# Values projected eight heads at a time, a second row chunk turned by TensorE, and another split of the exponentials

## The chip, the cores and the metric

The kernel runs on one core of one Trainium2 chip. The metric is device time in microseconds (us), from runs of the whole kernel. The core has a matrix engine (TensorE, PE in the profile), a vector engine (VectorE, DVE), a scalar engine (ScalarE, ACT), a general engine (GpSimd, POOL) and a sync engine whose queue issues most transfers (SyncE, SP). Tensors live in SBUF, 128 partitions wide; PE writes its results to PSUM, 8 banks of 512 float32 columns per partition.

## The reference, cut to what matters

The input x has 2048 rows of 512. Two attention layers read it, each with 32 heads of 16 columns, and a gate mixes them.

```python
g = sigmoid((x * gate_w).sum(-1, keepdims=True))
# A: linear attention with a feature map
phi(t) = concat(softmax(t @ w_phi), softmax(-t @ w_phi))     # per head, 16 -> 32
a = (phi(q) @ (phi(k).T @ v)) / (phi(q) @ sum(phi(k)) + 1e-6) @ A_wo
# B: softmax attention over all 2048 keys
b = softmax(q @ k.T * 0.25) @ v @ B_wo
return g * a + (1 - g) * b
```

Nearly all of the work is B's softmax: 32 heads x 2048 x 2048 exponentials.

## The kernel before, in words

**Sets and steps.** B is done in 32 sets: four chunks of 512 query rows, in each four groups of eight heads, in each group the even and the odd heads. A set goes through 16 tiles of 128 keys (a step each). For a step PE makes scores in two pairs of matmuls (L752), each pair 128 keys x 1024 columns in PSUM; then the scores are turned into exponentials, and PE multiplies these by the values (four matmuls of 32 columns of values, L794 or L807), summing in the PSUM tile O. The values of a head stand in `vB` as 16 columns and two columns of ones, so that the sum of the exponentials comes out beside the product.

**Two ways to an exponential.** On ACT one activation makes 1024 columns (L771), so a step costs two of them. On DVE a step is two conversions of scores to an integer form (L761, "di"), a mask (L777, "dm"), a multiply (L780, "dw") and a second mask (L784, "de"); the result is two parts, D's F and I tiles, and each is multiplied by the values. `NDVE` (L35) says for each of the 32 sets how many of its 16 steps DVE takes: 117 of 512 in all. In sets 0 and 1 it is one step each.

**What else is done.** Keys and queries of B are projected by groups of eight heads (`k_proj` L488, `q_proj` L500), four matmuls of 512 columns each (`fill`, L471, helper line L475), then copied out of PSUM. Queries are spread into four zero-padded copies: the first by four DVE multiplies with masks (L510), later ones by eight small transfers each on SP's queue (L521), into buffers that POOL clears at the start (L446). Values of B are projected for all 32 heads at once (`v_proj` L525): four matmuls of 512 columns for each tile of 128 rows, two tiles side by side in one of the three 1024-column PSUM tiles R, which the scores use too, and DVE copies both out at once (L469, 128x1024). All eight such pairs of tiles come before or in set 0 and early in set 1. A's part runs between: the gate (L593), folded weights (L613), phi of the keys for 16 row tiles (two ACT exponentials L634, a DVE sum L636 and reciprocal L640, a POOL multiply L641), then the products of keys and values (L665), then phi of the queries for 16 row tiles with numerator and denominator (L690 to L703). At the end of each set O is copied out (L828), turned by PE (L835) and divided (L840, L841). Output rows are made in `of`/`os` (L891, L899) and scaled (L907).

**The start.** x must stand transposed in SBUF as `xT`. Its first 512 rows come by a plain transfer (L405) and are turned by sixteen PE matmuls against an identity (L550); ACT copies one half out of PSUM (L553), DVE the other (L554). The other three chunks of 512 rows come by transposing transfers on SP's queue (L409), one after another. Weights come on ACT's queue in five transfers (L412 to L416), that of the values whole, in third place.

**What sets the order.** Every operation is added to a planner (`_Sched`, L90) with an engine, a priority, a duration of its own and what it depends on. `run` (L148) places operations one by one on a model of the engines; the order that comes out is the fixed program order of each engine, and waits on semaphores are put in from the dependencies. Priorities are times: `ut(u)` (L459) turns a place in the plan (32 units a set, 1024 in all) into a time, from `NDVE`. Constants such as `RUSH`, `HOLD`, `STAY`, `KLEAD`, `QLEAD`, `EARLY` (L47 to L61) shift priorities; `next_pe` (L117) picks PE's next operation, scores for ACT first when ACT has few ahead. Phi of the keys starts at unit 100, 16 units a tile (L648); the keys' products stand at 360, phi of the queries at 400, 32 units a tile (L681); output rows of a query chunk at 545 and on, 128 apart (L886).

Of the kernel before, what the change touches and what calls it, by code (L numbers as in the profile page):

```python
# [6 lines left out]
BF16 = mybir.dt.bfloat16  # L7
# [26 lines left out]
VROW = H * VW + 16  # L34
NDVE = [1, 1, 4, 4, 4, 3, 4, 4, 3, 4, 3, 4, 4, 3, 5, 4, 4, 3, 4, 3, 5, 3, 4, 4, 5, 3, 4, 4, 4, 3, 5, 4]  # L35
# [11 lines left out]
STAY = 1.0  # L47
PAIRS = (0, 1, 2, 3, 4, 5, 6, 7)
# [12 lines left out]
EARLY = 8.0  # L61
# [268 lines left out]
def _build(ctx, nc, A_x, A_wqkv, A_w_phi, A_wo, B_wqkv, B_wo, gate_w, out):  # L330
# [19 lines left out]
    vB_ = sb([128, NT, VROW], name="vB")  # L350
    vB = vB_[:, :, 0:H * VW].rearrange("p t (h c) -> p t h c", c=VW)
    vA = sb([128, NT, 8, 66], name="vA")
# [51 lines left out]
    xs = D_all[0].bitcast(BF16).rearrange("p (i c) -> p i c", c=D)  # L404
    op_x0 = dma("sp", -100, 3.6, xs, A_x[0, 0:NQ, :].rearrange("(i p) c -> p i c", p=128), name="x0")  # L405
    op_x = [None]
    for c in range(1, QC):
        op_x.append([add("sp", -100 + c, 2.5,
                         lambda e, c=c: e.dma_start_transpose(xT[:, :, NQ * c:NQ * (c + 1)], A_x[0, NQ * c:NQ * (c + 1), :]),  # L409
                         name=f"x{c}", dma=7.0)])  # L410
# [3 lines left out]
    op_wv = dma("act", -98, 6.0, W_Bv[:], wbv[:, :, 2 * D:3 * D], name="wv")  # L414
    op_wk1 = dma("act", -97, 8.0, W_Bk[:, :, 128:D], wbv[:, :, D + 128:2 * D], name="wk")
    op_wq1 = dma("act", -96, 8.0, W_Bq[:, :, 128:D], wbv[:, :, 128:D], name="wq")  # L416
    op_wat = add("sp", -90, 3.0, lambda e: e.dma_start_transpose(WAT[:], A_wqkv[:, 0:2 * D]), name="wat", dma=3.0)
# [22 lines left out]
    op_vpad = [pool(-99, 0.2, lambda e: e.memset(vB_[:, :, H * VW:VROW], 0.0), name="vpad")]  # L440
# [59 lines left out]
    def q_proj(g, c, prio, tile, off):  # L500
# [4 lines left out]
        if (g, c) == (0, 0):  # L505
# [3 lines left out]
            for j in range(4):  # L509
                ms.append(add("dve", prio + 0.01 * j, 0.39, lambda e, j=j: e.tensor_scalar(  # L510
                    qt.ap[:, j, :], q3(), masks[:, j:j + 1], None, op0=ALU.mult),
                    deps=[ev, op_masks] + (ms if j == 3 else []), tiles=[qt], name=f"qm{g}{c}{j}"))
            ev_q[g, c] = ms
# [11 lines left out]
    def v_proj(st, n, prio):  # L525

        tile = _Tile(M_r if n == 1 else R_r)
        fs = [fill(prio, tile, 512 * i, lambda t, i=i: xT[:, t, 128 * (st + i):128 * (st + i + 1)], lambda t: W_Bv[:, t, :],
                   op_x[st // 4] + [op_wv], f"vf{st}") for i in range(n)]
        use_wv.extend(fs)  # L530
        src = lambda: tile.ap[:, 0:512 * n].rearrange("p (t h d) -> p t h d", t=n, d=16)
        e1 = evac("dve", prio, lambda: vB[:, st:st + n, :, 0:16], src, fs, [tile], n=512 * n, name=f"vev{st}")
        for i in range(n):
            ev_v[st + i] = e1
# [7 lines left out]
    tx = _Tile(R_r)  # L542
    txv = lambda: tx.ap.bitcast(BF16).rearrange("p (t q) -> p t q", q=NQ)
    xtp = []
    for t in range(KT):

        def fn(e, t=t):
            ins = None
            for i in range(4):
                ins = e.transpose(txv()[:, t, 128 * i:128 * (i + 1)], xs[:, i, 128 * t:128 * (t + 1)], ident[:])  # L550
            return ins
        xtp.append(add("pe", -80 + t, 0.3, fn, deps=[op_x0, op_id], tiles=[tx], mode="full", name="xtp"))
    op_x[0] = [add("act", -80, 0.9, lambda e: e.copy(xT[:, 0:2, 0:NQ], txv()[:, 0:2, :]), deps=xtp[0:2], tiles=[tx], name="xev"),  # L553
               add("dve", -80, 0.6, lambda e: e.tensor_copy(xT[:, 2:4, 0:NQ], txv()[:, 2:4, :]), deps=xtp[2:4], tiles=[tx], name="xev")]  # L554
    I_r.tenant[0] = _Tile(None)
    I_r.tenant[0].ops = xtp
    tq = _Tile(R_r)
    k_proj(0, 0, -50, tq, 0, "act")
    q_proj(0, 0, -49, tq, 512)
    tk1 = _Tile(R_r)  # L560
# [4 lines left out]
    for st in range(0, NT, 2):  # L565
        if st // 2 in PAIRS:
            v_proj(st, 2, ut(2 * st) - VLEAD)
        else:
            v_proj(st, 1, ut(2 * st) + 0.5)
            v_proj(st + 1, 1, ut(2 * st + 2) + 0.5)  # L570
# [76 lines left out]
    for st in range(NT):  # L647
        prio = ut(100 + 16 * st)  # L648
# [9 lines left out]
    for lo, hi in ((0, 4), (4, 8)):  # L658
        tkv = _Tile(M_r)
        kvo = []  # L660
        for g in range(lo, hi):
# [6 lines left out]
            kvo.append(add("pe", ut(360 + 3 * g), 0.5, fn, deps=op_phk + ev_vA + kvo[-1:], tiles=[tkv], mode="full", name="kv"))  # L668
        kvw = lambda tkv=tkv: tkv.ap[:, 0:260].rearrange("p (g c) -> p g c", c=65)
        op_kz.append(add("dve", ut(384), 0.334, lambda e, kvw=kvw, lo=lo, hi=hi: e.tensor_tensor(  # L670
            kz[:, lo:hi, 0:64], kvw()[:, :, 0:64], mask64[:].unsqueeze(1).to_broadcast([128, 4, 64]), ALU.mult),
            deps=kvo + [op_m64], tiles=[tkv]))
        op_kz.append(add("dve", ut(384), 0.1, lambda e, kvw=kvw, lo=lo, hi=hi: e.tensor_tensor(
# [3 lines left out]
    op_woA = dma("sp", ut(400), 4.0, WoA, A_wo.rearrange("(t p) c -> p t c", p=128), deps=op_kz, name="woA")  # L677
    op_woB = dma("sp", ut(400), 4.0, WoB, B_wo.rearrange("(t p) c -> p t c", p=128), deps=op_kz, name="woB")
# [421 lines left out]
```

## Time and profile before

| what | value |
|---|---|
| median of 3 runs | 791.6 us (791.0 to 792.72) |
| the profiled execution's own time | 790.62 us |
| its span, first to last instruction | 788.8 us |
| ACT busy | 764.3 us, 97% of the span |
| DVE busy | 710.5 us, 90% |
| PE busy | 708.3 us, 90% |
| POOL busy | 121.1 us, 15% |
| mean granted clock of PE | 0.998 of full speed |
| scores to exponentials on ACT (L771) | 790 activations of 1024 columns |
| steps on DVE (L777, one each) | 117 |
| value projection: copies out of PSUM | 8, 1225 ns each |

Busy time counts each engine's own instructions, in one profiled execution; what an engine waits for is put down to the instruction whose end released it. Consecutive instructions of one engine overlap in their records, so that the time from one start to the next is shorter than one duration. The span leaves out 1.8 us of the execution's own time. A line number is a line of the kernel, and several operations recorded by one helper share its line.

### The profile page before, as it was taken

The numbers are of one execution on the slowest core, as the hardware profiler recorded it, in microseconds if no ns is written. First come the engines' busy times: TensorE is split into PE (matmuls) and PEld (weight loads), VectorE is DVE, ScalarE is ACT, GpSimd is POOL, SyncE is SP. The second block draws the span as 40 slices with busy tenths as digits, with TensorE's granted clock in tenths as the row PEclk, the third lists the DMA queues.
The fourth block names the chain that finished last, engine by engine and source line by source line (L and its number), as shares of the span: only waits on it lengthen the run. The fifth ranks groups of instructions, "written<-read, shape, count | busy, mean of one in ns | idle before, by whom it ended". The sixth has DMA issues, their size and how long they took to land.

```text
span 788.8 us, 13621 instructions
## 1 busy us (share of the span) xinstructions
PE 708.3 (90%) x5645; PEld 224.7 (28%) x5716; DVE 710.5 (90%) x883; ACT 764.3 (97%) x865; POOL 121.1 (15%) x123
## 2 busy tenths in 40 slices
PE   8899999999999898998888999899998999988886
PEld 3223232222222222332222323222232232222222
DVE  2456999999999999999999999999999999999993
ACT  4989999999999999999999999999999999999995
POOL 7000002022233322111112010310111101120000
PEclk9999999999999999999999999999999999999999
DMA  9100000000000000023110121210111101120000
GB/s 240 28 8 2 11 4 1 10 6 1 14 1 8 9 1 14 1 68 41 28 21 21 30 19 34 48 23 19 27 22 40 35 14 27 35 42 1 7 1 30
DMA packets 55923, 19.57 MB, mean 25 GB/s; under 512 B 48304, under 2 KB 55856, under 8 KB 55856
## 3 DMA queue, kind: packets, MB, share of 16 engines
q1 hardware_dynamic: 52960, 17.06, 10.4%
q10 hardware_dynamic: 2640, 1.57, 0.7%
q8 instruction: 46, 0.75, 0.4%
q14 instruction: 21, 0.17, 0.1%
q0 software_dynamic: 256, 0.02, 0.0%
HBM read 3.69 MB, written 2.10 MB: 7 GB/s over the span
## 4 chain that ended last, share of the span: by engine, by line
ACT 87%; PE 6%; DVE 4%; DMA 2%; SPq 1%; issue 0%
ACT E L771 80%; ACT WAT L634 4%; PE ps L752 2%; ACT phiK L771 2%; PE ps L475 1%; DVE D L761 1%; DMA xT<-in_A_x_dram 1%; ACT vA L771 1%; PE ps L891 1%; PE ps L807 1%; SPq L521 1%; DVE D L777 1%; DVE D L780 1%; SPq L409 1%; PE ps L665 0%; DMA WB<-WB 0%
## 5 line engine op out<-in xcount | busy, mean ns | idle before, releaser
L771 ACT ACTIVATE E<-ps 128x1024 bf16<-128x1024 f32 x766 | 713.2, 1185 | 4.3 <-PE ps L807 2.2
L752 PE MATMUL ps<-q,kT 64*128 64x512 bf16 x2048 | 362.8, 385 | 58.1 <-ACT E L771 45.7
L761 DVE TENSOR_SCALAR D<-ps 128x1024 int16<-128x1024 f32 x234 | 284.5, 1216 | 21.7 <-PE ps L752 21.1
L752 PEld LDWEIGHTS ps<-q,kT 64*128 64x128 bf16 x2048 | 89.8, 93 | 275.2 <-ACT E L771 214.3
L807 PE MATMUL ps<-E,vB 128*32 128x512 bf16 x1532 | 149.1, 389 | 5.0 <-issue 4.3
L780 DVE TENSOR_TENSOR D<-D 128x2048 bf16<-128x2048 bf16 x117 | 141.4, 1209 | 0.6
L794 PE MATMUL ps<-D,vB 128*32 128x512 bf16 x936 | 90.8, 386 | 1.6 <-issue 1.0
L638 POOL TENSOR_TENSOR acc<-acc,ss 128x64 f32<-128x64 f32 x32 | 24.9, 778 | 435.4 <-DVE ss L636 435.4
L777 DVE TENSOR_SCALAR D<-D 128x2048 int16<-128x2048 int16 x117 | 83.8, 717 | 1.1
L784 DVE TENSOR_SCALAR D<-D 128x2048 int16<-128x2048 int16 x117 | 81.7, 698 | 0.1
L807 PEld LDWEIGHTS ps<-E,vB 128*32 128x32 bf16 x1532 | 37.8, 93 | 85.4 <-issue 77.5
L475 PE MATMUL ps<-xT,WB 128*128 128x512 bf16 x111 | 40.2, 388 | 3.3 <-ACT WAT L634 1.4
L634 ACT ACTIVATE WAT<-ps 128x512 bf16<-128x512 f32 x64 | 39.6, 755 | 0.0
L636 DVE TENSOR_REDUCE ss<-WAT 128x64 f32<-128x1024 bf16 x32 | 38.8, 1212 | 0.6 <-ACT WAT L634 0.4
L475 PE MATMUL ps<-Wp,xT 128*128 128x512 bf16 x98 | 38.0, 389 | 0.5 <-DVE OT L469 0.3
L641 POOL TENSOR_TENSOR phiK<-WAT,ss 128x1024 bf16<-128x1024 bf16 x16 | 35.6, 2222 | 10.7 <-DVE ss L640 10.7
L641 POOL TENSOR_TENSOR WB<-WAT,ss 128x1024 bf16<-128x1024 bf16 x16 | 33.5, 2096 | 14.3 <-DVE ss L640 14.3
L794 PEld LDWEIGHTS ps<-D,vB 128*32 128x32 bf16 x936 | 23.7, 94 | 37.5 <-issue 29.0
L469 DVE CAST vB<-ps 128x1024 bf16<-128x1024 f32 x8 | 9.8, 1225 | 22.0 <-PE ps L475 22.0
L835 PE MATMUL ps<-ident,OT 128*128 128x128 f32 x128 | 27.6, 300 | 0.5 <-ACT WAT L634 0.3
L891 PE MATMUL ps<-phiK 128*128 128x512 bf16 x74 | 25.8, 386 | 0.8 <-issue 0.3
L848 POOL TENSOR_TENSOR acc<-acc,rB 128x64 f32<-128x64 f32 x8 | 5.1, 633 | 133.9 <-DVE rB L840 133.9
(98 smaller groups left out, 351.2 us busy)
## 6 DMA issues: line engine op xcount, KB each, us to landing
out_dram<-Wp SPq DMA_DIRECT2D x16, 128.0 KB, 1.7
q<-qs SPq DMA_DIRECT2D x120, 16.0 KB, 1.8
WB<-in_B_wqkv_dram ACTq DMA_DIRECT2D x2, 384.0 KB, 8.6
D<-in_A_x_dram SPq DMA_DIRECT2D x1, 512.0 KB, 4.5
WB<-in_B_wqkv_dram ACTq DMA_DIRECT2D x1, 512.0 KB, 6.8
WAv<-in_A_wqkv_dram SPq DMA_DIRECT2D x1, 512.0 KB, 4.1
phiK<-in_A_wo_dram SPq DMA_DIRECT2D x1, 512.0 KB, 4.0
phiK<-in_B_wo_dram SPq DMA_DIRECT2D x1, 512.0 KB, 4.8
```

Of the source, the lines that this page charges most:

```text
L475: f = add("pe", prio - rush + 0.01 * t, MM, lambda e, t=t: e.matmul(tile.ap[:, off:off + 512], lhsT=lhs(t), rhs=rhs(t), start=(t == 0), st ...
L634: o5 = [add("act", prio + 1, 0.478, lambda e, a=a: e.activation(ev()[:, :, a, :], P(), ACTF.Exp, scale=1.0 - 2.0 * a), deps=[f], tiles=[ti ...
L636: o6 = add("dve", prio + 5, 1.13, lambda e: e.tensor_reduce(ss.ap[:, 0, :], ee.ap.rearrange("p (g f) -> p g f", f=DH), AX.X, ALU.add), dep ...
L641: return add("pool", prio + 7, 1.95, lambda e: e.tensor_tensor(dst().rearrange("p (g f) -> p g f", f=DH), ee.ap.rearrange("p (g f) -> p g ...
L752: ins = e.matmul(r.ap[:, 512 * i:512 * (i + 1)], lhsT=kT[p0:p0 + 64, g, 128 * kt:128 * (kt + 1)], rhs=qt.ap[p0:p0 + 64, 2 * pair + par, :] ...
L761: last_di = [add("dve", when - 6, 1.133, lambda e, r=r, I=I, part=part: e.tensor_scalar(I.ap[:, 1024 * part:1024 * (part + 1)], r.ap, EXP_ ...
L771: exps.append(add("act", when, 0.904, lambda e, r=r, E=E: e.activation(E.ap, r.ap, ACTF.Exp, scale=EXP_SCALE), deps=[q], tiles=[r, E], nam ...
L777: d1 = add("dve", pd, 0.06 + 0.54 * nk, lambda e, I=I, F=F, n=n: e.tensor_scalar(F.ap[:, 0:n], I.ap[:, 0:n], 0x007F, 0x3F00, op0=ALU.bitwi ...
L780: d4 = [add("dve", pd + 0.01 * y, 1.133, lambda e, I=I, F=F, lo=2048 * y: e.tensor_tensor(F.ap[:, lo:lo + 2048].bitcast(BF16), I.ap[:, lo: ...
L784: d2 = add("dve", pd + 0.1, 0.06 + 0.54 * nk, lambda e, I=I, n=n: e.tensor_scalar(I.ap[:, 0:n], I.ap[:, 0:n], -128, 0x0001, op0=ALU.bitwis ...
L794: ins = e.matmul(O.ap[32 * s:32 * s + 32, :], lhsT=vB_[:, kt, VW * h:VW * h + 32], rhs=w.ap.bitcast(BF16)[:, base + 1024 * (s % 2) + 512 * ...
L807: ins = e.matmul(O.ap[32 * s:32 * s + 32, :], lhsT=vB_[:, kt, VW * h:VW * h + 32], rhs=es[s % 2].ap[:, 512 * (s // 2):512 * (s // 2 + 1)], ...
```

## The change

1. **Split of the exponentials.** `NDVE` is replaced: 120 steps on DVE in place of 117, 3 and 4 of them in sets 0 and 1 in place of 1 and 1, and in the other sets 113 in place of 115.
2. **Values by groups of eight heads.** `v_proj(g, c)` makes the values of eight heads for a chunk of 512 rows: sixteen matmuls of 128 columns into the one-bank PSUM tile M, and one copy of 512 columns. Group 0 stands ahead of set 0, each later group with the keys of its group. The weights of the values come in two transfers, 128 columns and 384. Since a value product reads 32 columns, 18 of them a head's, the groups stand in `vB` in reverse order, so that what is read past a group's last head belongs to the group before; a product therefore depends on its own group and on that one.
3. **Rows 512 to 1023 loaded plainly** and turned by PE like the first 512 (`turn`), with a second pair of copies on ACT and DVE; two transposing transfers are left.
4. **Masks of the first queries** in the order 0, 2, 1, 3, and a score pair waits for the one mask that it reads instead of two.
5. **Places in the plan.** Phi of the keys from unit 160 at 18 units a tile (100 at 16), its products at 450 (360), phi of the queries from 490 at 27 units a tile (400 at 32), output rows from 635, 108 apart (545, 128); other constants as listed.

```diff
-NDVE = [1, 1, 4, 4, 4, 3, 4, 4, 3, 4, 3, 4, 4, 3, 5, 4, 4, 3, 4, 3, 5, 3, 4, 4, 5, 3, 4, 4, 4, 3, 5, 4]
+GW = 8 * VW
+NDVE = [3, 4, 4, 4, 3, 3, 4, 4, 4, 3, 4, 4, 4, 3, 2, 5, 5, 3, 4, 4, 4, 2, 5, 4, 4, 3, 4, 4, 5, 3, 4, 4]
...
-STAY = 1.0
-RUSH = 1.5
-HOLD = 0.4
+STAY = 3.0
+RUSH = 2.0
+HOLD = 0.3
...
-RUSH_O = 25.0
-RUSH_1 = 8.0
-QLEAD1 = 28
+RUSH_O = 20.0
+RUSH_1 = 12.0
+QLEAD1 = 26
...
-VLEAD = 3.0
-KLEAD1 = 24
-KLEAD = 40
-QLEAD = 32
-EARLY = 8.0
+VLEAD = 4.0
+VLEAD1 = 32
+RUSH_V = 20.0
+PK0 = 160
+PKS = 18
+PQ0 = 490
+PQS = 27
+KLEAD1 = 32
+KLEAD = 32
+QLEAD = 40
+EARLY = 4
...
+    xs = [D_all[c].bitcast(BF16).rearrange("p (i c) -> p i c", c=D) for c in range(2)]
+    op_xs = [dma("sp", -100 + c, 4.0 + 4.3 * c, xs[c], A_x[0, NQ * c:NQ * (c + 1), :].rearrange("(i p) c -> p i c", p=128), name="x0")
+             for c in range(2)]
...
-    op_wv = dma("act", -98, 6.0, W_Bv[:], wbv[:, :, 2 * D:3 * D], name="wv")
+    op_wv0 = dma("act", -98, 5.0, W_Bv[:, :, 0:128], wbv[:, :, 2 * D:2 * D + 128], name="wv0")
...
+    op_wv1 = dma("act", -95, 10.0, W_Bv[:, :, 128:D], wbv[:, :, 2 * D + 128:3 * D], name="wv")
...
-            for j in range(4):
+            for n, j in enumerate((0, 2, 1, 3)):
...
+    def v_proj(g, c, prio):
+        tile = _Tile(M_r)
+        rush = RUSH_V if g else 0.0
+        fs = []
+        for i in range(4):
+            def fn(e, i=i):
+                ins = None
+                for t in range(KT):
+                    ins = e.matmul(tile.ap[:, 128 * i:128 * (i + 1)], lhsT=xT[:, t, 128 * (4 * c + i):128 * (4 * c + i + 1)],
+                                   rhs=W_Bv[:, t, 128 * g:128 * (g + 1)], start=(t == 0), stop=(t == KT - 1))
+                return ins
+            fs.append(add("pe", prio - rush + 0.01 * i, 0.24, fn, deps=op_x[c] + [op_wv1 if g else op_wv0], tiles=[tile], mode="full",
+                          name=f"vf{g}{c}", nb=max(0.0, prio - EARLY)))
+        use_wv.extend(fs)
+        ev_v[g, c] = evac("dve", prio - rush, lambda: vB[:, 4 * c:4 * c + 4, 8 * (KT - 1 - g):8 * (KT - g), 0:16],
+                          lambda: tile.ap.rearrange("p (t h d) -> p t h d", t=4, d=16), fs, [tile], name=f"vev{g}{c}")
...
+    turn(0)
     tq = _Tile(R_r)
     k_proj(0, 0, -50, tq, 0, "act")
     q_proj(0, 0, -49, tq, 512)
+    turn(1)
...
+    for c in range(QC):
+        v_proj(0, c, ut(8 * c) - VLEAD)
...
+            v_proj(g, c, ut(64 * g - VLEAD1 + 8 * c))
...
-        prio = ut(100 + 16 * st)
+        prio = ut(PK0 + PKS * st)
...
-        prio = ut(400 + 32 * st)
+        prio = ut(PQ0 + PQS * st)
...
-... deps=[ev_k[g, kt // 4]] + (ev_q[g, qc][pair * 2:pair * 2 + 2] if len(ev_q[g, qc]) > 1 else ev_q[g, qc]), ...
+... deps=[ev_k[g, kt // 4], ev_q[g, qc][(2 * pair + par) % len(ev_q[g, qc])]], ...
...
-                        due.append((at + 2, pv, exps + [ev_v[kt], op_vones], es + [O]))
+                        due.append((at + 2, pv, exps + [ev_v[g, kt // 4], ev_v[max(g - 1, 0), kt // 4], op_vones], es + [O]))
```

More of the change, by code (lines that the diff above doesn't have):

```diff
@@ L541, in _build, with turn, fn @@
             deps=[z0], tiles=[tw, tz], mode="full", name="warm")
[L542 to L556, printed above, removed]
+    def turn(c):
+        tx = _Tile(R_r)
+        txv = lambda: tx.ap.bitcast(BF16).rearrange("p (t q) -> p t q", q=NQ)
+        xtp = []
+        for t in range(KT):
+            def fn(e, t=t):
+                ins = None
+                for i in range(4):
+                    ins = e.transpose(txv()[:, t, 128 * i:128 * (i + 1)], xs[c][:, i, 128 * t:128 * (t + 1)], ident[:])
+                return ins
+            xtp.append(add("pe", -80 + t + 33.5 * c, 0.26, fn, deps=[op_xs[c], op_id], tiles=[tx], mode="full", name="xtp"))
+        sl = slice(NQ * c, NQ * (c + 1))
+        op_x[c] = [add("act", -80 + 34 * c, 0.9, lambda e: e.copy(xT[:, 0:2, sl], txv()[:, 0:2, :]), deps=xtp[0:2], tiles=[tx], name="xev"),
+                   add("dve", -80 + 34 * c, 0.6, lambda e: e.tensor_copy(xT[:, 2:4, sl], txv()[:, 2:4, :]), deps=xtp[2:4], tiles=[tx], name="xev")]
+        I_r.tenant[c] = _Tile(None)
+        I_r.tenant[c].ops = xtp
+    turn(0)
     tq = _Tile(R_r)
@@ L757, in _build @@
                         when = at + (part * 1.3 if vec else pair * 0.95)
[L758 removed]
+                        q = add("pe", when - (0.0 if vec else RUSH), 0.226, qk, deps=[ev_k[g, kt // 4], ev_q[g, qc][(2 * pair + par) % len(ev_q[g, qc])]], tiles=[r, qt], mode="row",
                                 name=f"qk{nset}.{kt}", feeds="dve" if vec else "act", after=last_di if vec else last_qk, nb=at - 2.0 if vec else 0.0)
```

63 lines of the change are left out of this document (23 added, 40 removed).

## The prediction, as it was put on record

> **What bounds the kernel now.** I read the page's busy table and slices first, then ScalarE's (ACT's) timeline at the start, the windows by stage, and the chain of waits.
>
> ```profile
> PE 708.3 (90%) x5645; PEld 224.7 (28%) x5716; DVE 710.5 (90%) x883; ACT 764.3 (97%) x865; POOL 121.1 (15%) x123
> ...
> DVE  2456999999999999999999999999999999999993
> ACT  4989999999999999999999999999999999999995
> ...
> L771 ACT ACTIVATE E<-ps 128x1024 bf16<-128x1024 f32 x766 | 713.2, 1185 | 4.3 <-PE ps L807 2.2
> ```
>
> ACT is busy 97% of the span, and its largest group, the exponentials, is idle for only 4.3 us in total. VectorE (DVE) is full too, except in the first four slices (2, 4, 5, 6 tenths of 19.7 us each): some 45 us lie free there. One exponential costs 0.917 us, not the mean of 1185 ns, in which neighbours overlap: the chain of waits has 88 of them in one piece of 80.68 us near the end. A phi pair on ACT (L634) is 0.98 us there.
>
> ACT's timeline over the first 50 us shows where it does wait:
>
> ```profile
> 6.04 1.01 ACT L553 COPY xT<-ps 128x1024 bf16<-128x1024 bf16 x1 [0.54 <-PE ps L550]
> 8.96 0.60 ACT L494 ACTIVATE kT<-ps 128x512 bf16<-128x512 f32 x1 [1.91 <-PE ps L475]
> 11.55 1.02 ACT L771 ACTIVATE phiK<-ps 128x1024 bf16<-128x1024 f32 x1 [1.99 <-PE ps L752]
> ...
> 20.35 10.21 ACT L771 ACTIVATE phiK<-ps 128x1024 bf16<-128x1024 f32 x11
> ...
> 47.02 1.02 ACT L771 ACTIVATE E<-ps 128x1024 bf16<-128x1024 f32 x1 [1.36 <-PE ps L807]
> ```
>
> Before 20.35 us only 5 exponentials are done; between 44 and 49 us another 2.15 us (0.32 + 1.36 + 0.47) are lost, where DVE stands in its row of value evacuations. From 50 us to the tail ACT loses 2.0 us in all. The windows (columns: stretch, its length, then busy time with count of PE, PEld, DVE, ACT, POOL; clock; DMA) show the spare room:
>
> ```profile
> 20.00:36.00 16.00, 14.22 (x85) 4.03 (x85) 7.52 (x8) 16.00 (x19) 0.00 (x0) 1.00 0.12 32
> 36.00:50.00 14.00, 13.50 (x90) 3.97 (x88) 5.08 (x5) 11.38 (x13) 0.67 (x1) 1.00 0.01 2
> ...
> 360.00:391.00 31.00, 26.27 (x232) 8.33 (x234) 30.89 (x40) 30.33 (x35) 5.20 (x4) 1.00 0.25 36
> ...
> 600.00:640.00 40.00, 37.55 (x306) 11.84 (x308) 39.81 (x52) 39.77 (x45) 4.28 (x6) 1.00 0.16 34
> ```
>
> From 20 to 50 us DVE is 42% busy while PE is 92% busy. Later DVE reaches 99.5%, and ACT still loses only 0.67 and 0.23 us in those stretches.
>
> **The part that is plain: 120 steps for 117.** A step moved to DVE takes two exponentials from ACT: 3 x 2 x 0.917 = -5.5 us. But the two lists differ in place: sets 0 and 1 go from 1+1 steps to 3+4 (-10 exponentials, -9.2 us), the other thirty from 115 to 113 (+4, +3.7 us). So the gain must be made in the first two sets, and I cost them apart.
>
> A step on DVE, from its chain of waits at 366 us:
>
> ```profile
> 366.41 1.13 DVE D L780
> 367.55 1.13 DVE D L761
> 368.68 0.60 DVE D L784
> 369.28 1.21 DVE D L761
> 370.49 0.60 DVE D L777
> ```
>
> that is 2 x 1.13 + 0.60 + 1.13 + 0.60 = 4.59 us.
>
> **Sets 0 and 1 before.** They hold 60 exponentials. 33 of them have begun before 48.52 us, 27 x 0.917 follow: they end at 73.4 us.
>
> **Sets 0 and 1 after, by ACT.** The second row chunk (512 to 1023) now comes plainly behind the first (which lands 4.5 us after its issue by the DMA list; half a megabyte more at the 300 GB/s that the DMA view shows around 6 us is about 2 us, so near 7.5 us, before PE asks at 10). PE, rid of the full-width value fills, does sixteen value matmuls for eight heads (9.0 to 10.0), then eight transposes, then the first score pair. ACT has one more copy (1.01 us by the row at 6.04), at about 10.8 to 11.8, and the first exponential follows at 11.8 against 11.55. The finer wait on the masks saves nothing here, since that copy stands in front. Only tiles 0 to 3 of the keys exist then, three of which go to DVE, so ACT makes two exponentials and waits for key chunk 1, which needs DVE's half of the new copy (to 12.6): key evacuation at 13.8, next exponential at 15.0. The transposed loads of chunks 2 and 3 start some 0.5 us later on SP than chunks 1 and 2 did (landing 10.58 and 14.49 by PE's wait), so about 11.5 and 15.5, each ahead of its use. From 15.0: 48 x 0.917 + two key evacuations of 0.5 = 45.0. ACT alone would end at **60.0 us**.
>
> **By PE.** From the built order, fills before the last score pair of set 1: before, 104 of 512 columns, 64 score pairs, 31 groups of four value products, and 4 + 4 + 16 small ones; after, 32 of 512, 128 value fills of 128 columns, 16 more transposes, 64 pairs, 32 groups. Prices are from:
>
> ```profile
> 5.40 1.05 PE L550 MATMUL ps<-ident,D 128*128 128x128 bf16 x16
> 7.24 1.90 PE L475 MATMUL ps<-xT,WB 128*128 128x512 bf16 x8 [0.79 <-DVE xT L554]
> ...
> 18.91 0.40 PE L807 MATMUL ps<-phiK,vB 128*32 128x512 bf16 x4
> 19.24 0.39 PE L752 MATMUL ps<-q,kT 64*128 64x512 bf16 x2
> 19.56 0.40 PE L807 MATMUL ps<-phiK,vB 128*32 128x512 bf16 x4
> ```
>
> 0.217 us for 512 columns ((1.90 - 0.385)/7), 0.055 for 128 ((1.05 - 0.22)/15), 0.33 for a value group and 0.32 for a score pair (start to start). Before: 22.6 + 20.5 + 10.2 + 1.8 = 55.1 us in the 66.2 between 7.24 and 73.4, so 11.1 of waits and changes of form. After: 6.9 + 7.9 + 20.5 + 10.6 = 45.9. With the same 11.1, set 1 ends at 64.2; with none it would be 53, and ACT's 60.0 counts. I take 62.5, a little nearer the upper end: PE has work in 92% of the time already, but the order groups the value fills into 17 blocks, fewer than the single fills it replaces. Gain: 73.4 - 62.5 = **10.9 us**, copy and start-up waits within it.
>
> The Trainium skill, "TensorE: Matmul & The Clock Gate", section Back-to-back issue gap, speaks against the finer fills: in a sustained stream of weight load and matmul, it says, 128 columns cost about 81 ns rather than the 56 of an isolated one. Here the sixteen transposes, each with its load, ran at 55 ns, so this trace sides with the lower figure; by 81 ns, as an estimate from that page, the 144 would cost 3.7 us more and the upper end would be near 68.
>
> **By DVE.** Up to that point it has 7 steps (32.1 us), 7 value evacuations of 0.60, 2 of keys, one each of queries and outputs (6.6 together): 38.7 from 12.6, so 51.3. Nine microseconds of cover for its waits. One wait is new: GpSimd clears three query buffers from 12.77 to 18.05 us, while DVE was idle, and the first step's L777 now falls there. The nearest row, DVE's and GpSimd's timelines:
>
> ```profile
> 385.75 2.25 POOL L641 TENSOR_TENSOR WB<-WAT,ss 128x1024 bf16<-128x1024 bf16 x1 [2.84 <-DVE ss L640]
> ```
> ```profile
> 386.13 2.42 DVE L777 TENSOR_SCALAR D<-D 128x2048 int16<-128x2048 int16 x1
> ```
>
> L777 took 2.42 instead of 0.68 and ended as GpSimd's operation did: 1.7 us lost. Between 0 and 5.3 (all three clears), I take 1.8, inside the cover: nothing on the path; without that cover, 1.8.
>
> **Sets 2 to 31.** +3.7 us of exponentials. Values of groups 2 and 3 move here: 128 fills x 0.055 = 7 us of PE and 8 x 0.60 = 4.8 us of DVE, in sets 2 to 6, while phi of the keys leaves sets 3 and 4 (about 3 x 1.6 us of DVE) and DVE has one step fewer. ACT's own wait there was none; I add nothing. The query phi is put closer (27 units of a 1024-unit plan per tile instead of 32, beginning at 490 instead of 400). In that half DVE has 65.5 steps = 300.6, 16 phi with their numerators at 2.62 (L636 1.13, L640 0.46, L693/L695 0.37, L703 0.66), 14 outputs at 0.66, 8 query evacuations, 16.7 set ends at 1.11 = 74.4: 375 us against ACT's 403 x 0.917 + 16 x 0.98 = 385.6, so 97.2%. Before, the same sum from unit 400 gave 427.5 of 448.5, 95.3%. It is tighter; cost 0 if DVE runs as at 600 us, 5 if as many waits remain as between 391 and 771 (DVE idle 11.4 of 380). I take **+1.0**. SP's queue gets no new transfers there; woA and woB only go later. The tail (last exponential at 777.4, span 788.8) has the same work: 0, give or take 1.
>
> **Sum:** -10.9 + 3.7 + 1.0 = -6.2 us on the profiled execution, 790.62 us (span 788.8 and 1.8 around it): 784.4. The runs' median, 791.6, lies 1.0 above it: **785.4**.
>
> **Rivals.**
> - *The start pays in full*: DVE and PE never hold ACT, set 1 ends at 60.0, the later half costs nothing: 791.6 - 13.4 + 3.7 = 782. For it: PE's ledger has 7 us of air. Against: PE was 92% busy from 20 to 50 us. Chance 0.17.
> - *PE is the bound of the start*: each of the 17 blocks costs a change of form on both sides (34 x 0.1 = 3.4 over the 62.5 to 64.2): set 1 ends at 66 to 67.5, 791.6 - 6.6 + 3.7 + 1 = 789.7. For it: a lone fill beside score pairs takes 0.32 instead of 0.217. Against: the fills replaced paid that too. Chance 0.16.
> - *DVE becomes the bound of the second half* (slower): if it cannot do better than the 94.6% it ran at there (427.5 in the 452 us from 325 to 777), 375 takes 396.4, 10.8 over ACT: 785.4 - 1 + 10.8 = 795. Breaking even needs 6.2 + 1 more than ACT, DVE at 95.5%. For it: every DVE delay now has less room to be made up. Against: 99.5% at 600 us with 0.23 lost. Chance 0.09.
> - *The moved loads come late* (chunk 1 plain, value weights in two parts of small rows): 2 to 3 us on PE's first stretch, 787 to 788.5; counted in the forecast's upper part.
>
> Forecast (783 to 788.5): 0.55; 0.03 for something not listed. Range **781.0 to 791.0**: it takes in the forecast, most of the first rival and the second. About 0.2% is what a measurement of this kernel can tell from no change, so 790.0 and 793.2 are the bounds: faster 0.55 + 0.17 + half of 0.16 = 0.80; same 0.11; slower 0.09.
>
> **What would show it.** Right: the 50th exponential ends near 62.5 us; 24 exponentials of the first sets run without a gap of 1 us after 15 us; ACT's row has 760 exponentials of E; DVE's first three slices read 6 or more. Wrong: a wait of ACT on PE in sets 0 and 1 summing to over 5 us; L777 near 15 us over 3 us long with ACT idle behind it; ACT idle by more than 4 us in the second half with PE or DVE as the releaser; the 128-column value fills at 80 ns or more each.

## The result, and the profile after

| what | before | after |
|---|---|---|
| median of 7 runs | 791.55 us (789.97 to 792.72) | 788.86 us (786.27 to 789.59) |
| ratio after to before | | 0.9957, 95% interval 0.9942 to 0.9972 |
| the profiled execution | 790.62 us, span 788.8 | 789.59 us, span 787.7 |
| last exponential of E ends | 777.4 us | 776.24 us |

The changed kernel is faster by 0.4%. The forecast of 785.4 us had the sign and the range (781 to 791) right, but the gain is 2.7 us where 6.2 were forecast, and the time lies just above the band of 783 to 788.5 that had the most weight. A second set of runs (run 1 below) put the same kernel at 786.48 us against 791.96, ratio 0.9943 (0.9922 to 0.9963). The size goes with PE's granted clock: over both sets, the four runs with a mean clock of 0.999 took 785.8 to 786.3 us, and the four with 0.993 or 0.994 took 789.1 to 790.4.

Two rows of slices (tenths of 19.7 us each) and the largest group of the profile after:

```profile
DVE  3899999899999999997999999989989999999993
ACT  3999999999999999999999999999999999999995
...
L792 ACT ACTIVATE E<-ps 128x1024 bf16<-128x1024 f32 x760 | 708.3, 1170 | 5.2 <-PE ps L773 4.9
```

DVE's second to fourth slices went from 4, 5, 6 to 8, 9, 9: the free time near the start is used. ACT makes six exponentials fewer and is still busy 97% of the span (760.5 us), so it is the bound as before. Its first slice fell from 4 to 3, and its idle time ahead of exponentials of E rose from 4.3 to 5.2 us. ACT's timeline after (start, us, then in brackets the idle time before it and what ended it) shows the first of the two losses:

```profile
0.73 5.83 ACTq L409 DMA_DIRECT2D WB<-in_B_wqkv_dram  x6
6.58 1.28 ACT L576 ACT_TABLE_LOAD   x1 [6.58 <-issue]
7.88 1.01 ACT L576 COPY xT<-ps 128x1024 bf16<-128x1024 bf16 x1
11.68 0.60 ACT L505 ACTIVATE kT<-ps 128x512 bf16<-128x512 f32 x1 [2.79 <-PE ps L486]
13.92 1.01 ACT L576 COPY xT<-ps 128x1024 bf16<-128x1024 bf16 x1 [1.65 <-PE ps L572]
14.83 1.95 ACT L792 ACTIVATE phiK<-ps 128x1024 bf16<-128x1024 f32 x2
...
40.04 26.10 ACT L792 ACTIVATE E<-ps 128x1024 bf16<-128x1024 f32 x28
```

ACT's first copy begins at 7.88 us instead of 6.04, because ACT's queue is still issuing transfers (L409): six of them take 5.83 us, where five took 3.46, and the sixth alone takes 2.23. The table load behind them takes 1.28 us in both kernels. PE's timeline shows what the late copy costs (before, the same eight projections took 1.90 us after a wait of 0.79):

```profile
8.99 3.08 PE L486 MATMUL ps<-xT,WB 128*128 128x512 bf16 x8 [2.04 <-issue]
```

The first exponential begins at 14.83, not at 11.55 as before. The second keys follow at 17.97. From 20.1 us on there is no gap, and 24 exponentials are done by 40.04; 26 more at 0.917 end set 1 at **63.9 us**, against 73.4 before. (The trace itself has the last exponential of set 1 begin at 62.96, and before at 72.85: 9.9 us apart and not 9.5. The prediction's 73.4 is 0.4 too early. The balance below keeps it; with the trace's times the start gains 0.4 more and the later sets lose 0.4 more.)

The second loss is late. PE's, ACT's and SP's timelines around 566 us after:

```profile
567.44 0.34 PE L711 MATMUL ps<-kz,WB 128*128 128x4 bf16 x8 [1.63 <-DMA WB<-WB]
```
```profile
568.14 3.77 ACT L792 ACTIVATE E<-ps 128x1024 bf16<-128x1024 f32 x4 [1.27 <-PE ps L773]
572.41 1.02 ACT L792 ACTIVATE E<-ps 128x1024 bf16<-128x1024 f32 x1 [0.50 <-PE ps L773]
```
```profile
557.98 5.95 SPq L532 DMA_DIRECT2D q<-qs  x8
563.97 1.31 SPq L705 DMA_TRANSPOSE WB<-WB  x1
```

The denominator of a query tile (L711) waits 1.63 us for the transposing transfer of phi (L705), with score pairs queued behind it on PE. That transfer was issued only at 563.97, after eight query splits (L532) had held SP's queue for 5.95 us, though POOL's phi product had ended at 558.29, 0.3 us after the splits began. The windows (stretch, length, PE, PEld, DVE, ACT, POOL busy, granted clock, DMA) show what followed each of PE's two waits (2.04 us before 8.99, and this one):

```profile
10.00:12.00 2.00, 2.00 (x7) 0.74 (x6) 0.00 (x0) 0.32 (x1) 0.00 (x0) 0.50 1.18 319
...
568.00:572.00 4.00, 3.62 (x29) 0.94 (x25) 4.00 (x7) 3.77 (x4) 0.00 (x0) 0.66 0.50 98
572.00:576.00 4.00, 4.00 (x19) 0.61 (x17) 2.10 (x4) 3.10 (x5) 0.00 (x0) 0.50 0.00 0
```

The granted clock fell to 0.50, and a score pair that takes 0.32 from start to start took 0.54 (571.76 to 572.30). So ACT lost not one wait but four around 566: 1.27 + 0.50 + 0.48 + 0.29 = 2.54 us.

**The balance.** Set 1 ends 9.5 us sooner (63.9 for 73.4). From there to the last exponential the kernel takes 712.3 us instead of 704.0, 8.3 more. The windows of these stretches give ACT 4.65 us more of busy time (four exponentials are 3.7 of it) and 3.7 us more of idle time (5.25 for 1.56). The tail is unchanged, 11.5 for 11.4. Together -9.5 + 8.3 + 0.1 = -1.1, as the spans say.

### The profile page after: what moved, and what is told of

It is laid out like the page before. It is cut to its first block, busy times and chain, and to the rows that moved or that the text cites. A ratio compares the mean times of both kernels' runs of the same rounds, so it can differ in the third digit from the quotient of the medians.

```text
span 787.7 us, 14149 instructions
## 1 busy us (share of the span) xinstructions
PE 733.8 (93%) x5936; PEld 236.7 (30%) x5936; DVE 726.3 (92%) x907; ACT 760.5 (97%) x860; POOL 115.4 (15%) x123
## 4 chain that ended last, share of the span: by engine, by line
ACT 77%; PE 13%; DVE 7%; SPq 1%; DMA 1%; issue 1%
ACT E L792 70%; PE ps L773 5%; ACT WAT L655 4%; DVE D L782 3%; PE ps L486 2%; ACT phiK L792 2%; PE ps L912 2%; PE ps L828 2%; SPq L532 1%; DVE D L801 1%; PE ps L815 1%; ACT vA L792 1%; DVE D L798 1%; PE ps L546 1%; PE ps L559 1%
## 5 line engine op out<-in xcount | busy, mean ns | idle before, releaser
L782 DVE TENSOR_SCALAR D<-ps 128x1024 int16<-128x1024 f32 x240 | 291.4, 1214 | 25.8 <-PE ps L773 24.8
L801 DVE TENSOR_TENSOR D<-D 128x2048 bf16<-128x2048 bf16 x120 | 146.7, 1223 | 0.8
L815 PE MATMUL ps<-D,vB 128*32 128x512 bf16 x960 | 94.3, 388 | 0.0
L659 POOL TENSOR_TENSOR acc<-acc,ss 128x64 f32<-128x64 f32 x32 | 19.3, 604 | 423.0 <-DVE ss L657 423.0
L486 PE MATMUL ps<-xT,WB 128*128 128x512 bf16 x128 | 48.4, 399 | 3.1 <-issue 2.0
L486 PE MATMUL ps<-Wp,xT 128*128 128x512 bf16 x128 | 49.9, 396 | 0.2
L912 PE MATMUL ps<-phiK 128*128 128x512 bf16 x88 | 30.2, 386 | 0.0
L486 PE MATMUL ps<-WAv,xT 128*128 128x512 bf16 x64 | 23.9, 389 | 1.5 <-ACT WAT L655 0.9
## 6 DMA issues: line engine op xcount, KB each, us to landing
WB<-in_B_wqkv_dram ACTq DMA_DIRECT2D x3, 384.0 KB, 10.2
```

The lines of the kernel that those rows point to most:

```text
L486: f = add("pe", prio - rush + 0.01 * t, MM, lambda e, t=t: e.matmul(tile.ap[:, off:off + 512], lhsT=lhs(t), rhs=rhs(t), start=(t == 0), st ...
L782: last_di = [add("dve", when - 6, 1.133, lambda e, r=r, I=I, part=part: e.tensor_scalar(I.ap[:, 1024 * part:1024 * (part + 1)], r.ap, EXP_ ...
L801: d4 = [add("dve", pd + 0.01 * y, 1.133, lambda e, I=I, F=F, lo=2048 * y: e.tensor_tensor(F.ap[:, lo:lo + 2048].bitcast(BF16), I.ap[:, lo: ...
L815: ins = e.matmul(O.ap[32 * s:32 * s + 32, :], lhsT=vB_[:, kt, vcol(h):vcol(h) + 32], rhs=w.ap.bitcast(BF16)[:, base + 1024 * (s % 2) + 512 ...
L912: f1 = add("pe", prio + 0.01 * k, MM, lambda e, tile=tile, off=off, k=k, qc=qc, sb_=sb_, lhs=lhs, rhs=rhs: e.matmul(tile.ap[:, off:off + 5 ...
```

## Experiments

The theory behind them: the change works where set 1 ends, as predicted, and what the sum missed is two waits: ACT's long issue at the start, and SP's order at 566 us, both made longer by PE's lower clock behind them. Rivals: the waits are made up later and cost nothing; or one part alone (the new split, the places in the plan, the turned chunk) explains the gain. Ratios are to the kernel before on the same chip. Some freeze every other engine's order and others let the planner place everything anew; this turned out to matter, and each says which.

**1. The changed kernel itself, once more**, as a base.

> The changed kernel unaltered, for a second profile and more times. Theory: two places lose time in its first profile. At the start the sixth transfer on ACT's queue makes ACT's first copy end at 8.9 us, PE stands idle for 2.0 us and is then granted half its clock until about 13 us, so the first exponential comes at 14.8; that should be here again. At 566 us PE idles 1.6 us for a transposed phi and is granted half its clock until 576, which costs ACT 2.5 us; whether the clock falls there again I do not know, since the times vary by 3 us between executions. Rival: both are chance of that one execution, and the first exponential comes before 13 us here. About 788.9 us by either.

Measured: 786.48 us, ratio 0.9943 (0.9922 to 0.9963). Six issues on ACT's queue took 5.92 us, the first exponential began at 14.59. PE waited only 0.88 us for the denominator at 566.59, its clock did not fall there, and ACT lost 0.53 us at that place instead of 2.54. So the late dip varies from execution to execution. The start is alike in these two; in runs 6 and 8, with the same six issues, it is not (see run 6).

**2. The weights of the values in one transfer**, all other orders as in the changed kernel.

```diff
-    op_wv0 = dma("act", -98, 5.0, W_Bv[:, :, 0:128], wbv[:, :, 2 * D:2 * D + 128], name="wv0")
+    op_wv0 = op_wv1 = dma("act", -98, 6.0, W_Bv[:], wbv[:, :, 2 * D:3 * D], name="wv")
...
-    op_wv1 = dma("act", -95, 10.0, W_Bv[:, :, 128:D], wbv[:, :, 2 * D + 128:3 * D], name="wv")
```

> The value weights come in one transfer of 512 columns in third place instead of 128 and 384, so that ACT's queue issues five transfers and not six; the order on every engine is otherwise the same. Theory (the sixth transfer holds ACT): the table load starts near 4.2 us instead of 6.6, the first copy near 6.0 instead of 7.9, PE idles under 1 us before the projections and keeps its full clock, first exponential at 11.8 to 12.5 instead of 14.8, and 2 to 3 us less in all: 786. Rival (the later start is the price of the second turned chunk or of its load): first exponential stays after 14 us, time within 0.5 us of the unaltered one.

> The kernel with the value weights in one transfer, once more, as the neighbour on the same chip for the swap on SyncE's queue. Both theories: 784.7 to 785.8 us, first exponential at 12.3 to 13.3 us, TensorE's denominator near 566 us waits 0.8 to 1.7 us.

Measured: 785.21 us, ratio 0.9917 (0.9903 to 0.9932), and 785.72, ratio 0.9925 (0.9909 to 0.9941), on another chip. PE's and ACT's timelines of the first of them:

```profile
7.38 0.39 PE L485 MATMUL ps<-xT,WB 128*128 128x512 bf16 x1 [0.79 <-DVE xT L576]
```
```profile
0.72 3.60 ACTq L409 DMA_DIRECT2D WB<-in_B_wqkv_dram  x5
...
6.18 1.01 ACT L575 COPY xT<-ps 128x1024 bf16<-128x1024 bf16 x1 [0.54 <-PE ps L571]
```

Five issues take 3.60 us, the copy begins at 6.18, PE's wait ahead of the projections is 0.79 and not 2.04 us, its clock stays at 1.00, and the first exponential begins at 12.51, 2.1 us sooner than in run 1. Some of the gain is paid back, since PE now waits 0.35 and 0.25 us for weights behind its first projection. At the end 1.3 us are left (785.21 for 786.48). The intervals of these two overlap; but the four sets of runs with one transfer (runs 2, 2 again, 9 and 11, without run 10, which loses elsewhere) have ratios of 0.9915 to 0.9926, and the two sets of the changed kernel 0.9943 and 0.9957. This is as the theory had it: splitting the value weights cost the start about two microseconds.

**3. Ten matmuls on zeros while PE waits for the first copies**, outputs unused, to hold the clock; every other order as in the changed kernel.

```diff
+    turned = list(I_r.tenant[0].ops)
...
+    order = sch.order["pe"]
+    where = order.index(turned[-1]) + 1
+    for i in range(10):
+        o = add("pe", 0, 0.217, lambda e: e.matmul(tw.ap, lhsT=tz.ap[:, 0:128], rhs=tz.ap[:, 0:512], start=True, stop=True), name="warm")
+        o.start = turned[-1].start + 0.001 * (i + 1)
+        order.insert(where + i, o)
```

> Ten more matmuls of zeros, written to a tile that is overwritten, stand on PE between the first sixteen transposes and the first projections; they add work and compute nothing; every order is otherwise the same. Theory (PE's idle time of 2 us there makes the clock fall): ACT's first copy still comes at 7.9, the projections start at about 9.0 to 9.3 but run at full clock, eight in 1.9 us instead of 3.1, first exponential at 12.8 to 13.3 instead of 14.8, time 1.5 to 2 us less: 787. Rival (the clock falls for another reason, or only the late copy counts): the projections take 3 us still, first exponential at 14.8 or later, time the same or longer.

Measured: 787.36 us, ratio 0.9946 (0.9927 to 0.9966). PE's timeline at the start, where the added matmuls stand from 7.36 to 9.5:

```profile
9.51 1.89 PE L486 MATMUL ps<-xT,WB 128*128 128x512 bf16 x8
```

The clock stayed at 1.00 from 6 to 14 us and the eight projections took 1.89 us, where run 1 took 3.22 and the profile after 3.08. So the slow projections were the clock's doing: the same instructions, same order, same copies (ACT's at 7.94). The first exponential came 0.9 us sooner (13.69). The whole time does not show it: it is 0.9 us above run 1's, with intervals that overlap, where 1.5 to 2 less was expected.

**4. The second row chunk by a transposing transfer again**, planned anew.

```diff
-    xs = [D_all[c].bitcast(BF16).rearrange("p (i c) -> p i c", c=D) for c in range(2)]
+    xs = [D_all[c].bitcast(BF16).rearrange("p (i c) -> p i c", c=D) for c in range(1)]
...
-    turn(1)
```

> Rows 512 to 1023 come by the transposing transfer again, without PE's turn and the two copies; all else as in the changed kernel (six transfers on ACT's queue). Theory: ACT's late copy and PE's fall of clock are there as well, since they come from ACT's queue; the first exponential comes at about 14 to 14.5 but the keys of chunk 1 not before 12, ACT saves a copy of 1.0 us; time within 1.5 us of the changed kernel, 787.5 to 790.5. Rival (the second turned chunk is what makes the start late): first exponential at 12 or before and 2 to 3 us less; or (it is what makes the start fast) 3 to 4 us more because the key chunks come 4 us later each.

Measured: 796.2 us, ratio 1.0061 (1.0046 to 1.0076). The first exponential began at 11.20 us, but ACT's waits in the new order are in other places:

```profile
131.38 49.61 ACT L791 ACTIVATE E<-ps 128x1024 bf16<-128x1024 f32 x54 [4.50 <-PE ps L772]
...
721.70 1.09 ACT L654 ACTIVATE WAT<-ps 128x512 bf16<-128x512 f32 x2 [4.00 <-PE ps L486]
```

With 2.74 us at 119.38 these are over 100 us from the part that was edited. The run measures a new plan, not the chunk. So the next one keeps the order.

**5. The same, with every other order kept**: the turn's operations are struck out of the orders and their waits handed on.

```diff
+    x1 = op_xs[1]
+    x1.fn = lambda e: e.dma_start_transpose(xT[:, :, NQ:2 * NQ], A_x[0, NQ:2 * NQ, :])
...
+    for ops in sch.order.values():
+        ops[:] = [o for o in ops if o not in gone]
```

> Rows 512 to 1023 come by the transposing transfer, PE's turn and the two copies are struck out of the program, and every engine keeps the changed kernel's order otherwise (the run that planned anew lost its time between 119 and 135 us and at 721 us, not at the start). Theory: without half a megabyte of plain load before them ACT's six issues take 4.5 us instead of 5.9, the first exponential comes at 11.2 instead of 14.6, the 16th ends at 30.3 instead of 32.6, and the whole takes about 2 us less than the unaltered one: 784 to 785. Rival (the turned chunk is what makes the start fast): key chunk 1 later than with the turn, the 16th exponential after 33 us, 788 or more.

Measured: 787.95 us, ratio 0.9951 (0.9934 to 0.9968), no different from the changed kernel. ACT's timeline:

```profile
17.11 0.60 ACT L505 ACTIVATE kT<-ps 128x512 bf16<-128x512 f32 x1 [4.03 <-PE ps L486]
```

The six issues took 4.49 us, the first exponential came at 11.14, 3.5 us sooner, and then ACT waited 4.03 us for the second keys, whose rows PE had to wait for (1.81 us, on the transfer, at 15.19), and the granted clock was 0.50 from 16 to 20 us. Their copy came at 17.11, where the profile after had 17.97, and the exponential behind it at 19.16 in both. The expectation that the chunk costs the start 2 us falls: turning it gives back about what it takes, since without it a wait of PE, and the low clock behind it, only stand elsewhere.

**6. The split of before (117 steps) in the changed kernel**, planned anew: `NDVE` of before, nothing else.

> The changed kernel with the old list of steps (117 on DVE, 1 and 1 in sets 0 and 1), planned anew; the rest as changed. Theory (ACT's count of exponentials sets the time): 6 more of 0.917 us, 5.5 us more than the unaltered changed kernel, which took 786.5 to 788.9: about 792 to 794, no better than the kernel before. Rival (the values by groups and the start bring the gain, the list little): within 1.5 us of the changed kernel.

Measured: 795.19 us, ratio 1.0052 (1.0037 to 1.0067): 8.7 more than run 1, where six exponentials are 5.5. Between 20 us and the last exponential ACT waits 6.3 us in sum, the longest 2.22 at 626.04 and 1.26 at 123.91. Its start, which the change of the list leaves as it was, is a second test of run 3. PE's timeline:

```profile
9.01 1.89 PE L486 MATMUL ps<-xT,WB 128*128 128x512 bf16 x8 [2.44 <-issue]
```

Here too six issues took 5.85 us and PE waited 2.44 us, as in run 1. But the clock stayed at 1.00, the projections took 1.89 us, and the first exponential began at 13.19, 1.4 us sooner than in run 1 without any filler. Run 8 has the same (1.89 and 13.19, behind a wait of 1.67). So 1.4 us of the late start are the clock's, and whether they are lost varies as the late dip does.

**7. The new split (120 steps) in the kernel before**, planned anew: `NDVE` alone.

> The kernel before with the new list of steps on VectorE alone (120 for 117; 3 and 4 instead of 1 and 1 in the first two sets), its order planned again; nothing else changed. Theory: the steps pay only because the values come by groups: in the kernel before, TensorE has 55.1 us of fills ahead of the end of set 1, and 73.4 us pass, so ten exponentials fewer on ScalarE leave that end near 73 (the 50th exponential of E between 70 and 75 us), ScalarE waits for TensorE by 5 us or more in the first 60 us, and the thirty other sets cost 3.7 more: 792 to 797 us. Rival, the list itself is the gain and the values' placement is not needed: set 1 ends near 64 and the time is 784 to 788.

Measured: 818.59 us, ratio 1.0338 (1.032 to 1.0356). The end of set 1 went the way of the theory and further, to 64.68 + 18 x 0.917 = 81.2 us. ACT's timeline, and windows around the wait:

```profile
64.68 16.73 ACT L771 ACTIVATE E<-ps 128x1024 bf16<-128x1024 f32 x18 [15.80 <-PE ps L807]
```
```profile
48.00:56.00 8.00, 7.29 (x46) 2.29 (x46) 7.36 (x8) 0.88 (x1) 0.00 (x0) 1.00 0.01 2
56.00:65.00 9.00, 7.73 (x60) 2.49 (x60) 8.48 (x11) 0.32 (x1) 0.08 (x1) 1.00 0.00 1
```

From 48 to 65 us PE is busy 15.0 of 17 us and DVE 15.8, with full-width value fills, their 1.22 us copies and steps, and ACT works for 1.2. So in this plan the longer list does not pay without the values by groups. The time is over 20 us above the theory's 792 to 797. About 8 of the 27 us of loss are there by the end of set 1; in the new order ACT waits another 12.3 us behind it, the longest 5.84 at 739.63.

**8. The old places in the plan** (phi of the keys from 100, of the queries from 400) in the changed kernel, planned anew.

```diff
-PK0 = 160
-PKS = 18
-PQ0 = 490
-PQS = 27
+PK0 = 100
+PKS = 16
+PQ0 = 400
+PQS = 32
```

> The changed kernel with the old places of phi (keys from 100 at 16 units, queries from 400 at 32, outputs after these), planned anew. Theory: the later places matter because values of groups 1 to 3 now stand in sets 1 to 5, where DVE and PE have no room for phi as well; ACT waits some 3 to 6 us in sets 2 to 6, time 790 to 793. Rival (the places matter little, since DVE's work is only moved): 786 to 789.

Measured: 810.74 us, ratio 1.0257 (1.024 to 1.0274). Both expectations were far too low. ACT waits 11.73 us at 171.29, 2.65 and 3.83 behind it and 3.79 at 735.95.

**9. The denominator at 566 us moved behind the next three score pairs on PE**, on top of run 2.

```diff
+    order = sch.order["pe"]
+    i = order.index(dens[7])
+    order[i:i + 4] = order[i + 1:i + 4] + [dens[7]]
```

> The version with the value weights in one transfer, and on PE the denominator of query tile 7 moved behind the three score pairs that follow it; all else in the same order. That denominator waits for a transposed phi, whose transfer stands on SP's queue behind eight query transfers (558 to 563 us). Theory: PE no longer idles 0.9 to 1.7 us there, its clock is not halved at 566 to 576 in any execution, ACT's waits there fall from 0.5 to 2.5 us to under 0.6, and the times spread less: median 784, against 785.2. Rival (the clock falls for another reason): it falls there in the profile still, or the time stays at 785.2.

Measured: 785.3 us, ratio 0.9926 (0.9914 to 0.9939): the same as run 2. In its profile the denominator did not wait, the clock stayed at 1.00, and ACT lost 0.54 us at 567.59 instead of 2.1 (1.53 + 0.54). The time does not show it.

**10. On SP's queue, phi's transposing transfer ahead of the query splits, in two places**, on top of run 2.

```diff
+    order = sch.order["sp"]
+    for o in phTs:
+        i = order.index(o)
+        if order[i - 1].name.startswith("qsp"):
+            order[i - 1], order[i] = order[i], order[i - 1]
```

> The kernel with the value weights in one transfer, and on SyncE's queue the transposing transfer of a query tile's phi goes ahead of the eight query splits in two places (tiles 7 and 12 or so, near 556 and 651 us); all other orders stay. Theory: TensorE's denominator at 565 to 568 us waits because its transfer stands behind eight splits of 5 to 6 us; with the places changed it waits under 0.4 us, the granted clock stays above 0.95 between 560 and 580, ScalarE's waits from 480 to 775 us sum to under 1.7 us (2.8 in the profile with the value weights in one transfer), and the time is 0.3 to 1.5 us under its neighbour without the swap: 783.7 to 785. Rival, the splits are needed as soon as the transfer or something else ends last there: a wait of over 0.8 us stays at 560 to 580, or moves to the score pairs behind the splits, and the time is that of the neighbour within 0.3 us, or above it.

Measured: 792.54 us, ratio 1.0018 (1.0006 to 1.0031), 6.8 above its neighbour (run 2 again, 785.72). SP's and ACT's timelines:

```profile
621.43 1.24 SPq L704 DMA_TRANSPOSE WB<-WB  x1
622.71 5.00 SPq L531 DMA_DIRECT2D q<-qs  x8
```
```profile
630.78 2.11 ACT L791 ACTIVATE E<-ps 128x1024 bf16<-128x1024 f32 x2 [6.82 <-PE ps L772]
```

The first swap did what it was for: the denominator at 563.78 did not wait. The second did harm. There the splits had been issued at 613.63 in run 2; now they stood behind a transfer whose phi came only at 621.4, and the score pairs that read the split queries waited for them. The clock behind fell to 0.54. The error was in the expectation, which did not ask when the second transfer's input was ready.

**11. The first swap alone** (tile 7, `for o in phTs[7:8]`).

> The kernel with the value weights in one transfer, with one of the two swaps of the run before: only the transposing transfer near 556 us goes ahead of the eight query splits; the place near 614 us, where the splits then waited for a phi product that came 8 us later and ScalarE lost 6.8 us at 630.8, stays as it was. Theory: the denominator at 564 us waits under 0.3 us, the granted clock stays at 1.00 from 556 to 576, ScalarE's waits from 480 to 775 us sum to at most 1.7 us, nothing new opens at 630, and the time is 783.9 to 785.2 (0.5 to 1.3 under 785.2 to 785.7 without the swap). Rival, the 1.1 us wait and the clock behind it cost nothing that is not made up later: 785.2 to 786 as without the swap, or a wait of over 0.8 us opens at the score pairs behind the late splits.

Measured: **784.13 us**, ratio 0.9915 (0.99 to 0.9931), the five runs between 783.9 and 785.21. PE's timeline:

```profile
563.15 0.35 PE L710 MATMUL ps<-kz,WB 128*128 128x4 bf16 x8
```

No wait stands beside it. From 480 us to the last exponential ACT waits 0.8 us in sum, where run 2 again had 2.2, and the stretch from the end of set 1 to the last exponential is 709.3 us, 3.0 less than in the profile after. The span is 782.1, 5.6 below it: 2.6 from the start (set 1 ends at 61.3) and the 3.0 of that stretch. The time is inside the theory's range (783.9 to 785.2), but its interval overlaps those of run 2. So the start's cost is shown by traces and by the times of four sets of runs together, and the late dip's by traces, with a time that agrees.

## Why the prediction was right or wrong, point by point

- **What bounds the kernel**: right. ACT is busy 97% after as before, and every version that was slower lost time in waits of ACT on PE.
- **The gain must be made in sets 0 and 1**: right. Set 1 ends 9.5 us sooner; 10.9 was forecast, and the rest costs.
- **That it needs the finer value fills**: in line with run 7, where the new split without them ends set 1 at 81.2 us. Since the plan of run 7 is new as well, this alone does not show it.
- **The 128-column fill at 0.055 us**: right. Sixteen in a row take 1.06 us in run 1, as the transposes did that the price came from. The 81 ns that the Trainium skill gives ("TensorE: Matmul & The Clock Gate", section Back-to-back issue gap) did not occur at the full clock.
- **PE's ledger as near bound, 64.2 us**: too careful. After the first exponential at 14.83 set 1 needed 49.1 us, where the forecast had 50.7 (11.8 to 62.5). ACT had no gap after 20.1 us, and PE was busy 15.12 of 16 us from 20 to 36. The rival of a change of form for each block, 66 to 67.5, did not come.
- **"The first exponential follows at 11.8 against 11.55"**: this step failed. It came at 14.83. The forecast took ACT's six issues as free and asked only when the transfers land; in fact six issues, with another half megabyte in flight, held ACT for 5.83 us, so the first copy came 1.84 us later than before, PE waited 2.04 us, and its clock halved for the projections (3.08 us for 1.90). Run 2 takes the first away, run 3 the last, and in runs 6 and 8, where the clock did not fall, the first exponential began at 13.19 behind the same six issues. The text listed "the moved loads come late" as 2 to 3 us of PE's first stretch: right in size, wrong in what was late.
- **L777 lengthened by POOL's clears, inside the cover**: right in kind. It took 0.92 us in place of 0.68, less than the 1.8 taken, and ACT did not wait behind it. The prediction's own row had L777 end with POOL's operation; it ended 0.55 us behind it (388.55 and 388.00), and so it did here (20.47 and 19.92).
- **The 50th exponential near 62.5 us**: 63.9, later by 1.4. Of three microseconds lost at the start, half was made up.
- **Sets 2 to 31, +3.7 + 1.0**: the 3.7 came, and the 1.0 was mis-sized. ACT's idle time there grew by 3.7 us, 2.5 of it in the dip at 566. Another 0.9 us is busy time of ACT: an exponential behind a wait takes 1.02 us and one in a row 0.917, and ACT's exponentials wait 12 times there instead of 3, which makes 9 x 0.10 = 0.9 as an estimate. The text read DVE as the engine that would be tight; the wait was on SP's queue, of which it said that "SP's queue gets no new transfers there". That was true of their number; it did not ask in what order they stand. A batch of splits of 5.95 us stands ahead of a transfer that PE needs. The kernel before has the same arrangement (splits at 502.40, the transfer at 508.20), and there PE waited 0.84 us for it (511.66) and kept its clock; now it is 1.63 us, and the clock fell.
- **The tail, 0**: right (11.5 for 11.4).
- **The slower rival, DVE as the bound of the second half, 795**: did not come. DVE is busy 39.13 of 40 us from 600 to 640, and ACT loses 0.06 there.

The sum: 1.4 at the start and 3.6 in sets 2 to 31 are 5.0 of the 5.1 us by which the span (787.7) stood above the forecast of 782.6. With both waits taken away (run 11) the span is 782.1 and the time 784.13: the forecast's size was that of the change without these two waits. That it is met so closely is in part luck, since set 1 then ends 1.2 us sooner than forecast (61.3 for 62.5) and the rest takes 0.6 more.

What stays open: how much the turned chunk, the places and the new split are worth each. The runs 4, 6, 7 and 8 were planned anew, and their waits show that such a plan, with constants set for another input, loses several microseconds on its own account. Only that they do not pay one by one in such plans is measured. Also open is why ACT's sixth issue takes longer with more bytes in flight.

## What to carry to other kernels

An issue on a compute engine's queue is work of that engine: when a change adds a transfer there, or puts more bytes in flight beside it, add the issue's own time ahead of the engine's first instruction. Where the order of a queue is rebuilt, look on each queue for a long batch of small transfers that stands ahead of a transfer that another engine awaits; but ask when that transfer's input is ready before swapping, since a transfer that waits holds all behind it. Where a planner fixes all orders, test a part with the other orders frozen, or the experiment measures the plan.

## What the runs showed of the hardware that was not expected

- **PE's clock goes by fixed stretches of 3.41 us, not by the length of one wait.** In every profile here PE's times at half clock, those at the very end apart, last 3.41 us or twice that, and within a profile all changes lie on one grid of 3.41 us. Two windows of the profile after on that grid:

```profile
6.11:9.52 3.41, 1.38 (x18) 0.99 (x16) 0.69 (x1) 2.29 (x2) 2.91 (x6) 1.00 1.26 210
9.53:12.93 3.40, 3.40 (x18) 1.83 (x15) 0.79 (x2) 0.60 (x1) 0.00 (x0) 0.50 1.18 315
```

In the stretch ahead of the fall PE was busy for 1.38 of 3.41 us, 40%. Over all the profiles, by their busy times of PE, each stretch at full clock with PE busy for less than 48% was followed by a fall, and none with more than 64%; between the two both occur. So the same wait can cost the clock or not, by where it lies on the grid. The clock fell with waits of 1.12 (run 3 near 566 and run 2 again at 565), 1.63 and 2.04 (after), 1.65 (run 2), 1.81 (run 5) and 2.44 us (run 1); it did not with 1.55 (run 4 at 13.19), 1.67 and 1.80 (run 8 at 9.02 and 167.99), 1.72 (run 7 at 14.74) and again 2.44 us (run 6, where the stretch that holds most of the wait had PE busy for 1.67 of 3.41 us). The Trainium skill, "TensorE: Matmul & The Clock Gate", section Part 1: The HAM clock gate (the "warmup" mystery), has the fall after an idle window of about 3.4 us, and a window that runs freely. The length and the free run agree with these traces. That the window has to be idle does not: a window with PE busy for 40% was enough.
- **A sixth issue on ACT's queue took over 2 us with a second plain load in flight.** Five issues took 3.46 to 3.95 us (before, and runs 2, 7, 9, 10 and 11), six 4.49 and 4.55 where the second row chunk came by a transposing transfer (runs 5 and 4), and six 5.83 to 5.92 where it came plainly (after, runs 1, 3, 6 and 8). The first three take 0.48, 0.61 and 0.53 us in all of them; the sixth takes 0.94 in run 5 and 2.23 in the profile after. The Trainium skill, "DMA: Bandwidth & Descriptors", section Issuing engines are not separate DMA queues, calls the issuing time usually small beside the transfer. For each one alone that is so here (2.25 us at most, in run 1, against medians of 6.3 and 10.2 from issue to landing for the 128 and 384 KB pieces of the weights); but the six in a row held ACT for 5.83 us.
